# Twelve tiny loads of x among the last large loads of a decode step

## The chip, the cores and the metric

The kernel runs on one core of a Trainium2 chip. The core has a matrix engine (TensorE, PE in the profile), three engines for element-wise work (VectorE, DVE; ScalarE, ACT; GpSimd, POOL), a sync engine (SyncE, SP) that here does nothing but issue loads, and 16 DMA engines that move bytes from the chip's memory into the on-chip buffer. The metric is the device time of one execution in microseconds (us), as a median over runs.

## What is computed

One token `x` of 576 numbers is normalised and sent through two branches, whose results are added to it.

```python
xn = _layernorm(x)
return x + _A_ref(xn, k_cache, v_cache, wq, wo) + _B_ref(xn, w_in, w_sp, b_sp, w_out)
```

Branch A is attention for one query: `q = xn @ wq` gives 32 heads of 128; there are 16 key/value heads, so two query heads share one; only the last 4,096 positions of the cache of 65,536 are looked at; the softmax of the scores weighs the values, and the result (4,096 numbers) is multiplied by `wo`. Branch B is a gated MLP: `z = gelu(xn @ w_in)` gives 4,608 numbers, the second half is normalised, scaled and shifted by two scalars, multiplied with the first half, and multiplied by `w_out`. All inputs are bf16.

Every weight and every key and value is used once. The kernel must read 16 MiB of keys, 16 MiB of values and some 17 MB of weights, 50.96 MB by the profile.

## The kernel before

**The loads.** All large loads are issued by SP, in the order in which the code lists them, and land in a ring of seven buffers (`ring`, 20,736 bytes in each of 128 partitions): `wq` in three pieces, the keys of two pairs of heads, `w_in` in three pieces, then keys and values in turn (`K[m]`, `V[m]`, 2 MiB each, for m of 0 to 7), then `w_out` in one load (`wout`, L95), then `wo` in five loads of 14, 9, 6, 2 and 1 of its 32 slices (L95 again). Every one of these loads fills 128 partitions with one contiguous piece each. A load into a ring buffer is issued when the load seven places before it has been consumed, so SP waits for PE or DVE before most of them. SP works strictly in order: what stands behind a waiting load waits too.

**Small loads.** ACT issues three small loads at the start (`xrow`, x as one row of 1,152 bytes; two scalars of 2 bytes into `spb`, side by side in one tile) and the store of the result at the end.

**Completion signals.** Each load tells of its landing through a semaphore. The semaphores named in the trace's records show eight of them, used in turn by all loads of SP and ACT in their order in the program. Before a load takes a semaphore that the eighth load before it used, its issuer waits until that earlier load has landed.

**The work between.** Keys are transposed on DVE (`kT`, L268), scores are made on PE (`S`, L277), the maximum, exponential and sum run on DVE and ACT (L298 to L321), and the weighted sum of the values on PE (`ops`, L344). This is done in four groups of four key/value heads. `zps` (L380) is branch B's first product. The tail is `out_mms` (L467): two accumulators `acc`, each over half of the 576 output columns, take 18 slices of `w_out` and then the 32 slices of `wo`, two multiplications a slice. Then `res` is copied out of the accumulators (L492, L493), and ACT stores it (L494).

The order of all instructions is that of the code (`manual_schedule`); nothing is moved by a planner. What sets the order around the change is SP's queue alone:

```python
wout_sb = load_n(B_w_out, NF, 0, NF, "wout")
wo_sb = []
for n in (14, 9, 6, 2, 1):
    wo_sb += load_n(A_wo, 32, len(wo_sb), n, "wo")
```

In the following, "wo14", "wo9", "wo6", "wo2" and "wo1" are these five loads, and V4 to V7 and K5 to K7 the last values and keys.

Of the kernel before, what the change touches and what calls it, by code (L numbers as in the profile page):

```python
# [9 lines left out]
BF16 = mybir.dt.bfloat16  # L10
# [29 lines left out]
def kernel(  # L40
# [14 lines left out]
    nc = tc.nc  # L55
# [5 lines left out]
    const = ctx.enter_context(tc.tile_pool(name="const", bufs=1))  # L61
# [10 lines left out]
    x_flat = A_x.flatten_outer_dims()  # L72


    def ring_tile(name, rows, width):
        t = ring.tile([P, SLOT], BF16, name=name, tag="ring")
        return t[:, 0:rows * width].rearrange("p (s c) -> p s c", c=width)
# [8 lines left out]
    def load_kv(src, m, name):  # L86

        t = ring.tile([P, SLOT], BF16, name=f"{name}{m}", tag="ring")
        v = t[:, 0:TP * DH]
        nc.sync.dma_start(v, src[0, 2 * m:2 * m + 2, SK - W:SK, :].rearrange("h (r t) d -> r h (t d)", t=TP))  # L90
        return v.rearrange("p (t d) -> p t d", d=DH)

    def load_n(src, per, lo, n, name):
        v = ring_tile(f"{name}{lo}", n, D)
        nc.sync.dma_start(v, src.rearrange("(p t) n -> p t n", t=per)[:, lo:lo + n, :])  # L95
        return [(lo + t, v[:, t, :]) for t in range(n)]
# [8 lines left out]
        V[m - 2] = load_kv(A_v_cache, m - 2, "v")  # L105
    for m in range(NP - 2, NP):
        V[m] = load_kv(A_v_cache, m, "v")
    wout_sb = load_n(B_w_out, NF, 0, NF, "wout")
    wo_sb = []
    for n in (14, 9, 6, 2, 1):  # L110
        wo_sb += load_n(A_wo, 32, len(wo_sb), n, "wo")


# [315 lines left out]
    for j in range(2 * NP):  # L429
        g, o = divmod(j, GK)  # L430
# [94 lines left out]
```

## Time and profile before

| what | value |
|---|---|
| median of 3 runs | 127.33 us (127.26 to 127.34) |
| span of the profiled execution, first to last instruction | 125.4 us |
| time of that execution outside its span | not recorded; the median is 1.9 us over the span |
| read from memory | 50.96 MB, 406 GB/s over the span |
| PE, DVE, ACT, POOL busy | 68.4, 78.5, 33.6, 7.9 us |
| loads issued by SP | 24, in 128 rows each, of 0.14 to 2.6 MB |
| DMA packets on SP's queue | 4,032 |

The profile shows one execution: the busy time of every engine, the span in 40 slices, the DMA queues, and the chain of work that ended last. Its DMA line gives the mean busy share of the 16 DMA engines, so a value a little under full can mean that all are nearly full or that some are done and others are not. Behind the views lie records of single DMA packets (start, duration, size, queue) and of every semaphore update; they do not name the DMA engine.

### The profile page before, as it was taken

The page shows a single profiled execution, that of the slowest core. Times are in us where ns is not written, and L with a number is a line of the kernel's source. Part 1 is how long each engine was busy: PE and PEld are TensorE (multiplying, and loading weights), DVE is VectorE, ACT ScalarE, POOL GpSimd, SP SyncE. Part 2 cuts the span into 40 slices and gives each one's busy share as a digit, 9 for nine tenths or more (in the row PEclk, how much of TensorE's full clock was granted, in tenths as well). Part 3 has the DMA queues.
Part 4 walks back from the last instruction along what each step waited for, and adds up shares of the span by engine and source line. Part 5 has one row for each costly group of instructions (what it writes and reads, how often), then busy time and mean ns, then how long its engine had stood idle before and what let it go on. Part 6 is the DMA issues. An engine that isn't in the chain of part 4 may idle for free.

```text
span 125.4 us, 1630 instructions
## 1 busy us (share of the span) xinstructions
PE 68.4 (55%) x626; PEld 31.4 (25%) x626; DVE 78.5 (63%) x150; ACT 33.6 (27%) x85; POOL 7.9 (6%) x27
## 2 busy tenths in 40 slices
PE   0034810398999668069257049639029811178862
PEld 0021110112699612014011012411003511024640
DVE  6853049997517595794798298899098967005001
ACT  4000030000072950000441940260860092920001
POOL 2991000000000000100000000000000000000000
PEclk9999995558975555959958977986955996557998
DMA  4999999999999999999999999999999999999960
GB/s 115 455 423 422 425 434 439 422 428 435 428 438 418 434 434 428 423 444 423 428 439 434 413 439 434 428 428 434 428 436 434 428 426 439 434 409 427 416 261 0
DMA packets 4047, 51.06 MB, mean 407 GB/s; under 512 B 454, under 2 KB 584, under 8 KB 840
## 3 DMA queue, kind: packets, MB, share of 16 engines
q1 hardware_dynamic: 4032, 50.96, 95.6%
q8 instruction: 5, 0.08, 0.2%
q14 instruction: 2, 0.02, 0.0%
q10 hardware_dynamic: 8, 0.00, 0.0%
HBM read 50.96 MB, written 0.00 MB: 406 GB/s over the span
## 4 chain that ended last, share of the span: by engine, by line
DMA 71%; PE 11%; DVE 11%; issue 2%; SPq 1%; ACT 1%
DMA k<-in_A_k_cache_dram 44%; DMA wo<-in_A_wo_dram 17%; DMA wq<-in_A_wq_dram 10%; DVE kT L268 6%; PE S L277 5%; PE ops L344 3%; DVE Qb L255 2%; PE qps L227 1%; PE acc L467 1%; DVE q_rep L238 1%; ACT q_rep L236 1%; DVE on L358 1%; PE lps L327 1%; SPq L83 1%; DVE om L354 1%
## 5 line engine op out<-in xcount | busy, mean ns | idle before, releaser
L277 PE MATMUL S<-kT,Qb 128*8 128x512 bf16 x128 | 32.3, 636 | 30.3 <-DVE kT L268 30.3
L268 DVE STREAM_TRANSPOSE kT<-k 128x1024 f32<-128x1024 f32 x32 | 36.9, 1212 | 8.3 <-DMA k<-in_A_k_cache_dram 8.3
L305 ACT ACTIVATE pz<-S,nm 64x1024 bf16<-64x1024 f32 x8 | 11.2, 1406 | 45.0 <-DVE nm L301 30.3
L321 ACT COPY PT<-pt 32x64 f32<-32x64 f32 x64 | 18.9, 295 | 14.6 <-DVE pt L315 13.8
L277 PEld LDWEIGHTS <-Qb 128*8 128x8 bf16 x128 | 6.4, 96 | 49.7 <-issue 46.7
L344 PE MATMUL ops<-v,PT 128*16 128x512 bf16 x128 | 11.7, 441 | 3.5 <-ACT PT L321 3.5
L315 DVE STREAM_TRANSPOSE pt<-pz 128x1024 bf16<-128x1024 bf16 x8 | 9.4, 1212 | 4.1 <-ACT pz L305 4.1
L380 PEld LDWEIGHTS <-win 128*128 128x128 bf16 x162 | 10.1, 165 | 0.9 <-issue 0.9
L380 PE MATMUL zps<-XT,win 128*128 128x2 bf16 x162 | 10.2, 201 | 0.0
L354 DVE SCALAR_TENSOR_TENSOR om<-ops,rs,dmask 128x512 f32<-128x512 f32 x4 | 3.0, 742 | 7.4 <-PE ops L344 7.3
L298 DVE TENSOR_REDUCE mx<-S 128x1 f32<-128x1024 f32 x4 | 4.9, 1220 | 3.7 <-PE S L277 3.7
L344 PEld LDWEIGHTS <-PT 128*16 128x16 bf16 x128 | 5.0, 97 | 7.3 <-ACT PT L321 4.1
L227 PE MATMUL qps<-wq,XT 128*2 128x512 bf16 x36 | 4.2, 621 | 2.3 <-DVE XT L218 1.9
L467 PE MATMUL acc<-wo,Y 128*1 128x288 bf16 x64 | 4.6, 285 | 1.3 <-DMA wo<-in_A_wo_dram 1.3
L236 ACT CAST q_rep<-qps 128x512 bf16<-128x512 f32 x2 | 1.2, 585 | 14.0 <-DVE q_rep L238 14.0
L238 DVE CAST q_rep<-qps 128x512 bf16<-128x512 f32 x2 | 1.4, 692 | 5.1 <-PE qps L227 4.5
L193 PE MATMUL ps_x<-ones_b,xtw 1*128 1x1 bf16 x9 | 0.4, 162 | 7.2 <-DVE xtw L191 7.2
L492 DVE CAST res<-acc 1x288 bf16<-1x288 f32 x1 | 0.4, 446 | 6.1 <-PE acc L467 6.1
L358 DVE TENSOR_REDUCE on<-om 128x128 f32<-128x512 f32 x4 | 4.1, 1034 | 0.1
L327 PE MATMUL lps<-lx,lsum 128*128 128x1 f32 x8 | 2.1, 333 | 3.2 <-DVE Y L372 3.2
L493 ACT CAST res<-acc 1x288 bf16<-1x288 f32 x1 | 0.4, 389 | 12.4 <-PE acc L467 12.4
L467 PEld LDWEIGHTS <-Y 128*1 128x1 bf16 x64 | 2.9, 83 | 3.0 <-issue 1.9
(90 smaller groups left out, 46.8 us busy)
## 6 DMA issues: line engine op xcount, KB each, us to landing
k<-in_A_k_cache_dram SPq DMA_DIRECT2D x8, 2048.0 KB, 27.2
v<-in_A_v_cache_dram SPq DMA_DIRECT2D x8, 2048.0 KB, 27.8
win<-in_B_w_in_dram SPq DMA_DIRECT2D x3, 1728.0 KB, 27.1
wout<-in_B_w_out_dram SPq DMA_DIRECT2D x1, 2592.0 KB, 30.2
wq<-in_A_wq_dram SPq DMA_DIRECT2D x1, 2048.0 KB, 9.3
wo<-in_A_wo_dram SPq DMA_DIRECT2D x1, 2016.0 KB
wq<-in_A_wq_dram SPq DMA_DIRECT2D x1, 1536.0 KB, 12.5
wo<-in_A_wo_dram SPq DMA_DIRECT2D x1, 1296.0 KB
```

Of the source, the lines that this page charges most:

```text
L227: nc.tensor.matmul(qps[32 * g:32 * g + 2, :], lhsT=XT[:, s, :], rhs=wv[:, 512 * g:512 * (g + 1)], start=(s == 0), stop=(s == NS - 1), tile ...
L268: nc.vector.transpose(dst[:, 1024 * n:1024 * (n + 1)], src[:, 1024 * n:1024 * (n + 1)])
L277: nc.tensor.matmul(S[g % 2][32 * i:32 * i + 8, hf, :], lhsT=Qb[:, 2 * m + hd, be].rearrange("p a h -> p (a h)"), rhs=kv[:, be // 2, be % 2 ...
L298: nc.vector.tensor_reduce(out=mx[:, 0:1], in_=s[:], op=ALU.max, axis=mybir.AxisListType.XY)
L305: nc.scalar.activation(p[lo:hi, :, :, hd], s[lo:hi].rearrange("p a (t r) -> p (a t) r", r=16), ACT.Exp, bias=nm[lo:hi, 0:1], scale=SCALE, ...
L315: nc.vector.transpose(dst[:, 1024 * n:1024 * (n + 1)], src[:, 1024 * n:1024 * (n + 1)])
L321: nc.scalar.copy(PT4[32 * a:32 * a + 32, i % 2, i // 2, :], pt4[32 * i:32 * i + 32, :, a])
L344: nc.tensor.matmul(ops[32 * q:32 * q + 16, :], lhsT=d["PT"][:, pr, t0:t0 + 4].rearrange("p t x h -> p (t x h)"), rhs=V[2 * g + pr][:, t0:t ...
L354: nc.vector.scalar_tensor_tensor(out=om[:].rearrange("p c d -> p (c d)"), in0=ops[:], scalar=d["rs"][:, 0:1], in1=dmask[:].rearrange("p c ...
L358: nc.vector.reduce_sum(on[:], om[:].rearrange("p c d -> p d c"), axis=AXX)
L380: nc.tensor.matmul(zps[:, :, t], lhsT=wt[:, t, :], rhs=XT[:, s, :], start=(s == 0 and t == 0), stop=(s == NS - 1 and t == NF - 1), skip_gr ...
L467: nc.tensor.matmul(acc[n], lhsT=lhs[:, col:col + 1], rhs=wv[:, CW * n:CW * (n + 1)], start=False, stop=last, tile_position=(0, 32 * n))
```

## The change

A tile `mk` of 16 partitions is added, and twelve loads that fill parts of it from `x`. A load "of k rows" cuts the first k(23 + k) numbers of x into k rows of 23 + k numbers, and writes them into k partitions, at a column of their own. They are issued on SP's queue: those of 15, 14 and 13 rows ahead of `wout`; those of 12, 11, 10 and 9 between `wout` and wo14; those of 8, 7, 6, 4 and 2 between wo14 and wo9. Nothing reads `mk`. They hold 111 rows and 7,516 bytes together, and a row has 50 to 76 bytes.

```diff
     for m in range(NP - 2, NP):
         V[m] = load_kv(A_v_cache, m, "v")
+    mk = const.tile([16, 16 * 40], BF16, name="mk")
+
+    def rows_of_x(ks):
+        for k in ks:
+            n = 23 + k
+            nc.sync.dma_start(mk[0:k, 40 * k:40 * k + n], x_flat[:, 0:k * n].rearrange("o (k n) -> (o k) n", n=n))
+
+    rows_of_x((15, 14, 13))
     wout_sb = load_n(B_w_out, NF, 0, NF, "wout")
-    wo_sb = []
-    for n in (14, 9, 6, 2, 1):
+    rows_of_x((12, 11, 10, 9))
+    wo_sb = load_n(A_wo, 32, 0, 14, "wo")
+    rows_of_x((8, 7, 6, 4, 2))
+    for n in (9, 6, 2, 1):
         wo_sb += load_n(A_wo, 32, len(wo_sb), n, "wo")
```

## The prediction

> **What bounds the kernel now.** I read the page's slices and queues first, then the chain that ended last.
>
> ```profile
> DMA  4999999999999999999999999999999999999960
> q1 hardware_dynamic: 4032, 50.96, 95.6%
> q8 instruction: 5, 0.08, 0.2%
> q10 hardware_dynamic: 8, 0.00, 0.0%
> DMA 71%; PE 11%; DVE 11%; issue 2%; SPq 1%; ACT 1%
> ```
>
> The DMA engines are full from the second slice to the last but two; SP's queue (q1) alone takes 95.6% of them. No compute engine is near that, so the time is bytes over rate, plus a head and a tail. The tail is the place of the change, so I cut it finely (columns: stretch, length, busy time of PE, PEld, DVE, ACT, POOL, clock, DMA share, GB/s).
>
> ```profile
> 100.00:110.00 10.00, 1.77 (x16) 0.92 (x12) 5.00 (x10) 7.00 (x18) 0.00 (x0) 0.71 1.01 432
> ...
> 120.50:121.00 0.50, 0.23 (x4) 0.03 (x1) 0.00 (x0) 0.00 (x0) 0.00 (x0) 1.00 0.88 321
> 121.00:121.20 0.20, 0.00 (x0) 0.00 (x0) 0.00 (x0) 0.00 (x0) 0.00 (x0) 1.00 0.30 110
> 121.20:121.60 0.40, 0.07 (x2) 0.07 (x3) 0.00 (x0) 0.00 (x0) 0.00 (x0) 1.00 0.33 127
> 121.60:122.00 0.40, 0.40 (x8) 0.28 (x9) 0.00 (x0) 0.00 (x0) 0.00 (x0) 1.00 0.25 92
> 122.00:122.30 0.30, 0.30 (x10) 0.18 (x6) 0.00 (x0) 0.00 (x0) 0.00 (x0) 1.00 0.18 61
> ```
>
> From 121.0 on, about a quarter to a third of the DMA engines still work: eleven are done and five are late. The records of single packets say who. The 16 completions of the last load, wo1, arrive at 120.88 to 121.52 for eleven engines, at 121.92 for one and at 122.45, 122.53, 122.55 and 122.62 for four. Followed back, each late engine lost its time in one step, when an instruction fetch ran on it: the 16 KB fetches at 32.4, 42.9, 70.2 and 102.3 cost their engines some 0.95 us each, and smaller ones some 0.3. PE starts its last pair of multiplications at 122.66, 0.04 us behind the last completion. So **four late DMA engines set the end, and eleven have about 1.1 us to spare**.
>
> ```profile
> 100.24 21.25 DMA wo<-in_A_wo_dram
> 121.49 0.04 issue
> 121.53 1.46 PE acc L467 x18
> 122.99 0.43 DVE res L492
> ```
>
> This chain leaves the DMA with wo6's landing, at 121.49, but inside its PE piece PE waits for wo2 and wo1 too.
>
> **The change part by part.** Nothing is removed. Added are 12 loads (111 rows, 7,516 bytes), and `wout` and the five `wo` loads move behind them on SP's queue. ACT's and POOL's queues are not touched, though ACT's last store takes its semaphore in a later turn.
>
> *Time on the DMA engines.* The nearest rows are ACT's scalars of 2 bytes, which ran between the packets of a full engine. There, 16,384-byte packets follow each other every 607 ns, and every 613 where one small packet came between, data or completion alike: 6 ns a packet. A row of 68 bytes adds 68 / 27.0 GB/s (16,384 bytes in 607 ns) = 2.5 ns. So a row and a completion cost 6 + 2.5 + 6 = 14.5 ns on its engine. How a load of 15 rows is divided over engines no row shows. If all ran on one late engine, 123 packets x 6 ns + 7,516 bytes / 27.0 = 0.74 + 0.28 = 1.0 us at the end; if all ran on early engines, nothing, under their 1.1 us. I take the even division, because every large load puts 9 packets on each of 16 engines: 111 / 16 = 7 rows x 14.5 ns = **0.10 us**, on the late engines too, and so at the end. A dearer packet is possible: ACT's row of 1,152 bytes took 47 ns up to its completion; with that price, 47 + 6 = 53 ns x 12 loads = 0.64 us on an engine that takes part in all.
>
> The Trainium skill, "DMA: Bandwidth & Descriptors", section "Why a DMA increments its semaphore by 16 and not by 1", says that a load of k rows (k up to 16) runs on the lowest-numbered k engines. By it engines 0 and 1 would take 12 rows each, 0.17 us, and engine 15 none; the end would move by 0 to 0.17, by the numbers of the late engines, which no record here gives. Engine 0 by that rule is the one with ACT's single-row packets, and in this trace it is the second earliest at wo1, 1.27 us ahead of the last: the rule makes the forecast's cost smaller if anything.
>
> *Issue on SP.* Small loads on ACT cost 0.21 and 0.27 us of issue, the first one 0.51.
>
> ```profile
> 0.74 0.51 ACTq L115 DMA_DIRECT2D xrow<-in_A_x_dram  x1
> 1.28 0.21 ACTq L117 DMA_DIRECT2D spb<-in_B_w_sp_dram  x1
> 1.52 0.27 ACTq L118 DMA_DIRECT2D spb<-in_B_b_sp_dram  x1
> ```
>
> With 0.3 each, waits' overhead included, 12 cost 3.6 us of SP, which has nothing else to do; the cover is the backlog of the queue, from issue to landing 20 us and more. If it were gone, the 3.6 us would lie on the path.
>
> *New waits.* Eight semaphores go round over the loads. `win`'s second load shows the price: its ring buffer was free, and yet SP waited 1.4 us, for `wq`'s first load, eight loads before.
>
> ```profile
> SPq L83 <- DMA wq<-in_A_wq_dram: 1.4, 1, 1.4
> SPq L95 <- DMA k<-in_A_k_cache_dram: 4.7, 1, 4.7
> ```
>
> Twelve more loads in the round put each large load eight places behind a much younger one. I count on: the 15, 14 and 13 rows wait for K5, V3 and K6, landed by 81.13, so they go at 81.4; `wout` waits for V4 (85.97, before: issued at 81.39); 12, 11, 10 and 9 rows wait for K7, V5, V6 and V7 (90.8, 95.7, 100.5, 105.39); wo14 goes at 105.8 (before 85.80); 6 rows wait for `wout` itself (111.58); after them and the 4 and 2 rows, three issues of 0.3, wo9 goes at 112.5 (before 95.52) and wo6 at 112.9; wo2 waits for wo14 (116.35), and wo1 follows at 116.8 (before 113.88). An issue reaches the engines 0.9 to 1.0 us after it begins (`xrow` 0.74 to 1.64, `wq` 0.73 to 1.73). Needed, on the earliest engine, are: wo14 at 109.5, wo9 at 114.3, wo6 at 117.4, wo2 at 119.5, wo1 at 120.4. The closest is wo9: 113.4 against 114.3, **0.9 us to spare**; wo14 has 2.8, wo2 2.1 and wo1 2.6. Nobody but the loads waits for SP, so these waits cost 0.
>
> Other parts: the 1.3 KB of `mk` in the buffer and the ACT store's turn cost 0; the store's semaphore was last used by the 7 rows, landed 6 us before it.
>
> The sum is 0.10 us. The profiled span is 125.43, the median 1.90 above it; what lies around the span doesn't change, so 125.53 in the profile and **127.43** in the median.
>
> **The rivals.**
>
> *Dearer packets.* Up to 53 ns a load on engines that do nothing between: +0.3 to +0.64, 127.6 to 128.0. For it: no trace has 15 engines reading the same 1,152 bytes at once, and three completions in a row on one ring. Against: 2-byte packets cost 6 ns beside a full stream. The even load's whole gain is lost from 0.25 us on, that is 36 ns a load on a late engine with seven.
>
> *SP too late.* If a small load costs SP far more than on ACT, wo9 comes late. A late engine needs wo9 at 116.0; an early one that starts it at 116.2 ends with them (it needs 6.1 us to the end). So it decides from 116.2, an issue at 115.3, 3.7 us after `wout`'s landing: 1.2 us for each small load. At 1.5 us each the end moves by 0.9: 128.2.
>
> *One after the other.* If each small load has to land before the next is issued (one tile `mk`), twelve latencies come into the queue; the store's 1.1 us (123.50 to 124.60) x 12 gives up to 13 us, 140. Against it: the two loads into `spb` were issued 0.24 us apart, the first landing at 5.25. The same page, in its section "Rules for kernel authors", calls transfers under 64 KB mostly overhead, and gives some 2 us of fixed cost to each; by it 12 in turn would be 24 us. The trace shows such latencies to overlap.
>
> *Faster.* If the 16 engines share a limit, the early ones' time on small packets is the late ones' gain: their lag of 1.1 us would shrink. It decides from 0.25 us over the last 37 us, 0.7% in pace, 607 to 603 ns a packet. At a third of the lag: 126.95. Against it: a late engine's 2,304-byte packets follow at 89 ns both with 16 engines at work and with five.
>
> **How the numbers follow.** Forecast 0.48, dearer packets 0.22, SP late 0.12, one after the other 0.06, faster 0.12. 0.2% (0.25 us) is about what a measurement of this kernel can tell from no change. The forecast lies within it, and a fifth of the dearer packets: same 0.52; slower 0.18 + 0.12 + 0.06 = 0.36; faster 0.12. The range leaves out the serial case and most of the faster one, and ends above SP late at 1.5 us a load: 127.15 to 128.3. The forecast's own is 127.33 to 127.55.
>
> **What would show it.** After: 12 more issues on SP, `wout` issued near 86, wo14 near 105.8, wo9 near 112.5, wo1 near 116.8; DMA share still 1.01 until 120; 111 packets under 100 bytes of some 9 ns; the eleven-and-five picture 0.1 us later. A DMA share under 0.98 between 105 and 119 would be SP late; a late group that moves by over 0.25 us with full engines is dearer packets. The prediction is wrong if a wait I did not count holds SP, or if instruction fetches fall on other engines.

## The result, and the profile after

The changed kernel takes 127.99 us (127.79 to 128.14, 4 runs) against 127.30 (127.24 to 127.34, 4 runs) of the kernel before: a ratio of 1.0055, 95% interval 1.0039 to 1.0071. It is slower by 0.69 us, inside the stated range, but beyond the forecast of 127.43, which was "no change that can be measured". In the experiments below, one run of e6 (129.56 us), over 1.5% above the fastest of its kernel, counts as slow and is left out of its ratio.

The page of the changed kernel, its slices and queues and the shares of the chain that ended last:

```profile
span 125.9 us, 1642 instructions
DMA  3999999999999999999999999999999999999960
q1 hardware_dynamic: 4254, 50.96, 95.5%
DMA 78%; DVE 8%; PE 8%; SPq 2%; issue 2%; ACT 1%
```

The DMA engines are as full as before. SP issues 28 loads before (the table above says 24; 28 x 144 packets make its 4,032) and 40 after. SP's queue has 222 packets more, twice 111: each row came with a completion of its own. The end of the transfers, cut as before:

```profile
120.50:121.00 0.50, 0.47 (x8) 0.19 (x5) 0.00 (x0) 0.00 (x0) 0.00 (x0) 1.00 1.00 389
121.00:121.20 0.20, 0.00 (x0) 0.00 (x0) 0.00 (x0) 0.00 (x0) 0.00 (x0) 1.00 0.94 357
121.20:121.60 0.40, 0.00 (x0) 0.00 (x0) 0.00 (x0) 0.00 (x0) 0.00 (x0) 1.00 0.58 202
121.60:122.00 0.40, 0.23 (x4) 0.17 (x5) 0.00 (x0) 0.00 (x0) 0.00 (x0) 1.00 0.26 104
122.00:122.30 0.30, 0.30 (x10) 0.21 (x6) 0.00 (x0) 0.00 (x0) 0.00 (x0) 1.00 0.28 100
```

The early eleven engines, done at 121.0 before, now work on to 121.4, but from 121.6 on the picture is that of before: a quarter of the engines is late. wo1's last completion came at 122.78, 0.16 later than the 122.62 of before. The span grew by 0.43 (125.43 to 125.86), and the median by 0.69. So 0.27 of the loss lies between the last load and the last instruction, and 0.26 outside the span altogether; the other 0.16 is wo1's lateness, which is taken up again below.

The 0.27 is seen in SP's checks at the end of the program, the same kind of row in both kernels (times are those of the first and last start). First before, then after:

```profile
L520 SPq EVENT_SEMAPHORE  x7: 17/28/825, 119.4 to 125.4; - x7
```

```profile
L530 SPq EVENT_SEMAPHORE  x7: 17/28/28, 124.8 to 125.8; - x7
```

By the semaphore records, SP checks the eight load semaphores and two others at its end, in five instructions, two in each, in the same order in both kernels. Each that follows another costs 0.065 us. Before, the store of the result used the semaphore that is checked last: four checks were done from 119.4 on, while the last loads landed, and only the store's own was left. With twelve more loads in the round, the store takes the semaphore that is checked first. SP stands there until 124.78 and does the four other checks behind it. From the store's landing to the end of the span it took 0.83 us before (124.60 to 125.43) and 1.10 after (124.76 to 125.86).

### The profile page after: what moved, and what is told of

It reads as the page before. It is cut to its first block, busy times and chain, and to the rows that moved or that the text cites. A ratio compares the mean times of both kernels' runs of the same rounds, so it can differ in the third digit from the quotient of the medians.

```text
span 125.9 us, 1642 instructions
## 1 busy us (share of the span) xinstructions
PE 68.3 (54%) x626; PEld 31.5 (25%) x626; DVE 78.5 (62%) x150; ACT 33.6 (27%) x85; POOL 7.9 (6%) x27
## 4 chain that ended last, share of the span: by engine, by line
DMA 78%; DVE 8%; PE 8%; SPq 2%; issue 2%; ACT 1%
DMA k<-in_A_k_cache_dram 21%; DMA wout<-in_B_w_out_dram 20%; DMA v<-in_A_v_cache_dram 20%; DMA wq<-in_A_wq_dram 10%; DMA wo<-in_A_wo_dram 7%; DVE kT L278 5%; PE S L287 3%; DVE Qb L265 2%; PE ops L354 2%; PE qps L237 1%; DVE q_rep L248 1%; PE acc L477 1%; ACT q_rep L246 1%; SPq L113 1%; SPq L83 1%
## 5 line engine op out<-in xcount | busy, mean ns | idle before, releaser
L331 ACT COPY PT<-pt 32x64 f32<-32x64 f32 x64 | 18.9, 295 | 14.5 <-DVE pt L325 13.7
```

The lines of the kernel that those rows point to most:

```text
L331: nc.scalar.copy(PT4[32 * a:32 * a + 32, i % 2, i // 2, :], pt4[32 * i:32 * i + 32, :, a])
```

## The experiments

All put loads of the same pieces of x into `mk` (one of them takes rows of `w_out`). "Behind the store" is the number of checks that follow the one of the store; "end" is from the store's landing to the end of the span in the profiled run; "outside" is time less span, the mean over the runs.

| kernel | small loads on SP | behind the store | end | outside | median | ratio (95%) |
|---|---|---|---|---|---|---|
| before, again (e1) | 0 | 0 | 0.84 | 1.81 | 127.32 | 0.9996 (0.9987 to 1.0005) |
| the change | 12 | 4 | 1.10 | 2.08 | 127.99 | 1.0055 (1.0039 to 1.0071) |
| e2, one row each | 12 | 4 | 1.09 | 2.08 | 127.87 | 1.0060 (1.0035 to 1.0085) |
| e3, one row each | 8 | 0 | 0.83 | 1.82 | 127.44 | 1.0004 (0.9996 to 1.0013) |
| e4, 15 to 8 rows | 8 | 0 | 0.83 | 1.83 | 127.35 | 1.0003 (0.9994 to 1.0011) |
| e5, one row each | 4 | 4 | 1.09 | 1.83 | 127.60 | 1.0022 (1.0013 to 1.0031) |
| e6, the change and 4 early | 16 | 0 | 0.83 | 1.85 | 127.60 | 1.0028 (1.0012 to 1.0045) |
| e7, 128 rows each | 8 | 0 | 0.83 | 1.82 | 128.01 | 1.0057 (1.0044 to 1.0069) |
| e8, the change, 4 moved early | 12 | 4 | 1.10 | 2.09 | 127.90 | 1.0047 (1.0033 to 1.0060) |
| e9, one row each | 14 | 2 | 0.95 | 2.11 | 127.79 | 1.0033 (1.0021 to 1.0046) |
| e10, nine ahead of wo9 | 16 | 0 | 0.83 | 1.84 | 131.41 | 1.0317 (1.0296 to 1.0339) |
| e11, four more on ACT | 8 | 4 | 1.09 | 1.80 | 128.76 | 1.0120 (1.0097 to 1.0142) |
| e12, one row each | 10 | 3 | 1.00 | 1.84 | 127.47 | 1.0011 (1.0002 to 1.0020) |

### Packets, checks or a late queue?

The kernel before once more (no edit), for its spans:

> The kernel before once more, beside itself, for the span of each run. If the time outside the span is the same in both kernels (2.05 to 2.1 us in the runs of the changed kernel, 127.95 - 125.9 among them), the spans here are 125.2 to 125.3; if the changed kernel also pays outside its span, they are 125.4 and 1.9 lies outside. Ratio 1.000.

All twelve loads in their places, but of one row, and the same with eight of them; then the change with eight:

```diff
-            nc.sync.dma_start(mk[0:k, 40 * k:40 * k + n], x_flat[:, 0:k * n].rearrange("o (k n) -> (o k) n", n=n))
+            nc.sync.dma_start(mk[0:1, 40 * k:40 * k + n], x_flat[:, 0:n])     # e2, e3
...
-    rows_of_x((8, 7, 6, 4, 2))
+    rows_of_x((8,))     # e3, e4
```

> The twelve loads at the same places, but each of one row, so all their packets run on one engine, which is an early one. Theory A (the row packets on late engines cost 0.1 us, and the store's semaphore, now checked first of five at the end, costs 0.27): the last large load lands as before, the end still takes 1.10 us from the store's landing, so +0.27 in the span, 127.6. Theory B (all of the loss is the packets on the late engines): 127.3. Theory C (SP's late issue of wo9 costs the loss): as the changed kernel, 128.0.

> As the run before with the last four loads left out, so that the store's semaphore is again the last that is checked, and wo9 goes on SP right behind wo14. Theory A: 0.83 us from the store's landing to the end, 127.3 to 127.35. Theory B: 127.3. Theory C: 127.3. A cost per added load, wherever it lies: two thirds of what twelve cost.

> The changed kernel with the loads of 7, 6, 4 and 2 rows left out: the store's semaphore is the last one checked, wo9 is early, and the late engines have 1 to 8 small loads each. Theory A: +0.08 for packets, nothing at the end, 127.4. Theory B: nearly all of the loss stays, since nearly all packets stay (92 of 111 rows): 127.85. Theory C: 127.3.

e2 keeps nearly all of the loss (127.87) with 12 row packets instead of 111; e4 loses nothing that can be measured with 92 rows. So the rows are not the loss: theory B falls. Theory A's 1.10 and 0.83 us came as expected, but e2 stands 0.27 above its 127.6. That is the time outside the span: 2.08 us in e2 and in the change, 1.81 in the kernel before. I had taken it for fixed.

### The store's turn alone, and the time outside the span

e5 is e2 with only the 15, 14, 13 and 12 (as one row each); e6 is the change and four one-row loads behind the keys' fourth to seventh load:

```diff
         K[m] = load_kv(A_k_cache, m, "k")
+        if m in (3, 4, 5, 6):
+            k = (5, 3, 1, 0)[m - 3]
+            nc.sync.dma_start(mk[0:1, 40 * k:40 * k + 23 + k], x_flat[:, 0:23 + k])
```

> Only four one-row loads (ahead of wout three, behind it one). Nothing of them runs on a late engine, wo9 goes on SP behind wo14 at once, but the store takes the semaphore that is checked first of five at the end, as with twelve. Theory A1 (the store's turn is the whole loss): 1.10 us from the store's landing to the end of the span, and 2.05 outside it, so 127.8 as with twelve. Theory A2 (the turn costs 0.27 in the span, and the 0.2 outside it goes with the number of loads or of SP's instructions): 127.55. Theory D (the loss goes with the number of loads alone, none up to eight): 127.3.

> The whole change (twelve loads, 111 rows, wo9 as late on SP) and four one-row loads more, one each behind the keys' fourth to seventh load, so that the store again takes the semaphore that is checked last. Theory A1: all but the packets' 0.1 us comes back, 127.4. Theory A2: 127.6. Theory C (SP's late issue of wo9) or D (number of loads): 128.0 or more.

Both agree with A2 in the store's turn. Four one-row loads at a harmless place cost 0.29 us (127.60 against 127.31), and nearly all of it is the checks. Sixteen loads (e6), the whole change among them, bring the store back to the last check, and the end with it; the time outside came back too. That e6's median is still the 127.6 of A2 is chance: A2 put 0.2 us of it outside the span, and in e6 it lies inside. Without its three runs above 128 the median is 127.49. The checks of e5, e6 and e4, one row of each profile:

```profile
L529 SPq EVENT_SEMAPHORE  x7: 17/28/28, 124.7 to 125.7; - x7
```

```profile
L532 SPq EVENT_SEMAPHORE  x7: 17/28/825, 119.6 to 125.5; - x7
```

```profile
L530 SPq EVENT_SEMAPHORE  x7: 17/28/825, 119.6 to 125.5; - x7
```

Where the first check starts at 124.7, the store holds it and four stand behind; where it starts at 119.6, they were done while loads landed.

The outside time did not follow A2's "number of loads": 1.85 with sixteen, 2.08 with twelve. Four runs went after it. e8 moves four of the twelve loads (7, 6, 4 and 2 rows) behind the keys' fourth to seventh load; e9 and e12 have e3's eight and six or two one-row loads among the keys; e11 has e3's eight and four on ACT's queue:

```diff
     nc.scalar.dma_start(spb[:, 1:2], B_b_sp.flatten_outer_dims()[0:1, 0:1])
+    for k in (7, 6, 4, 2):
+        nc.scalar.dma_start(mk[0:1, 40 * k:40 * k + 23 + k], x_flat[:, 0:23 + k])
```

> All twelve loads of the change, but the 7, 6, 4 and 2 rows one each behind the keys' fourth to seventh load, so that wo9 goes on SP behind wo14 at once. The store's semaphore is checked first of five, as in the change. Theory A3 (in the span: 0.27 for the store's turn, 0.1 for packets; outside the span 0.25 that belongs to twelve loads): 127.9, with 2.07 outside, and no run far above the others. Theory E (the 0.25 outside comes from where the loads stand, or from SP's late issue): 127.65, with 1.82 outside. Theory C2 (SP's late issue of wo9 is what gives runs of 128.5 to 129.7): none here.

> Fourteen one-row loads, eight at places of the change and six one each behind the keys' third to eighth load. The store takes the third of the five checks, so two stand behind it: 0.83 + 2 x 0.065 = 0.96 us from its landing to the end, 127.45 if 1.82 lies outside the span. If the time outside grows from twelve loads on, 2.07 outside and 127.7; if it belongs to twelve alone, 1.82 to 1.85.

> Twelve one-row loads, eight on SP's queue at places of the change and four on ACT's queue at the start. The store's semaphore is checked first of five: 1.10 us from its landing to the end of the span. Theory G (the 0.25 outside the span goes with the length of SP's program): 1.82 outside, 127.6. Theory H (it goes with the number of loads, whoever issues them): 2.08 outside, 127.85.

> Ten one-row loads on SP's queue, two of them behind the keys' fifth and sixth load. The store takes the second of the five checks, three stand behind it: 0.83 + 3 x 0.065 = 1.03 us from its landing to the end. Outside the span 1.82 if the step comes between ten and twelve loads (127.5), 2.08 if between eight and ten (127.75).

The time outside is 1.80 to 1.85 with 0, 4, 8, 10 and 16 added loads on SP, and 2.08 to 2.11 with 12 and 14, wherever they stand (e8) and whatever their rows (e2). With eight on SP and four on ACT it is 1.80 (e11): so it goes with the loads that SP itself issues, not with the number of all loads. The records of e6, e9 and e10 (16, 14 and 16) hold one 8 KB instruction fetch more, 1.6 to 1.9 us behind the end of the span; those with fewer loads hold none there.

The semaphore records narrow the place. In the 0.37 us ahead of the span they are alike in all kernels, and the last one stands 1.90 to 1.91 us behind the span's end in the kernel before, e1, the change, e2 and e8. So the 0.26 lies behind that last one, or more than 0.37 ahead of the span. One group of them, the updates of semaphores 207 to 255, starts 0.65 to 0.66 us behind the end with 0 to 10 added loads on SP, 0.68 to 0.69 with 12 and 14, and 1.19 to 1.21 with 16, where the last updates come no later for it. So one step behind the span does move with the number of loads on SP. A wait of SP for the next block of its program would fit, but no row shows it, and no run made SP's program longer without adding loads: it stays an argument. The Trainium skill, "Runtime: NRT & Kernel Launch", section "Instruction fetch mechanics", says that programs are fetched in blocks while the current one runs, and that crossing a boundary is mostly hidden. Whether the 0.26 us is such a crossing no run here shows; the instruction fetches in the records are of 8 KB on one queue and of 16 KB on another.

The ends of e9 and e12, 0.95 and 1.00 us with two and three checks behind the store, lie near 0.83 + 0.065 each (0.96 and 1.03). Four places of the store (0, 2, 3 and 4 checks behind it) thus show the price of a check.

e11 held a surprise: it lost 1.1 us more than the checks cost. The four loads on ACT shift the round, so that `wq`'s third load comes eight places behind its first. SP's waits in the first 10 us of e11:

```profile
SPq L83 <- DMA wq<-in_A_wq_dram: 3.0, 1, 3.0
SPq L83 <- DMA xrow<-in_A_x_dram: 1.0, 1, 1.0
```

That load was issued at 5.50 instead of 1.62 and landed at 15.26 instead of 14.07, and the queue ran at 370 GB/s between 5 and 10 us, where it ran at 418 before.

### What does a packet cost, and a late load?

e7 has eight loads of 128 rows of 76 bytes at e4's places, so that all 16 engines carry 8 rows and a completion of each:

```diff
-            nc.sync.dma_start(mk[0:k, 40 * k:40 * k + n], x_flat[:, 0:k * n].rearrange("o (k n) -> (o k) n", n=n))
+            nc.sync.dma_start(mk[:, 40 * k:40 * k + 38], B_w_out[0:128, 0:38])
```

> Eight loads at the places of eight of the twelve, each of 128 rows of 76 bytes (from w_out), so that each of the 16 engines, the late ones too, has 8 rows and a completion of each load. The store's semaphore is the last one checked. By the prices of the trace, (8 x (6 + 2.8) + 6) ns = 76 ns a load, 0.6 us for eight, all at the end: 127.9. If a packet of this kind costs more than its time in the stream, over that; if the late engines do not set the end, 127.3.

It took 128.01, +0.70, 88 ns a load where 76 were worked out. From V7's landing to wo1's, the mean of the four latest completions grew from 17.19 to 17.21 us (the runs with no or one-row loads) to 17.80: 0.60, or 75 ns a load. Packets on the late engines do come out at the end, at about the price of the stream.

e10 puts nine one-row loads between wo14 and wo9:

```diff
-    rows_of_x((8, 7, 6, 4, 2))
+    rows_of_x((8, 7, 6, 5, 4, 3, 2, 1, 0))     # one row each, as in e2
```

> Nine one-row loads between wo14 and wo9, so wo9 stands eight places behind wo14 itself or nearly so, and one small load before it has to wait for wo14's landing (116.4): wo9 is issued at about 116.8. The store's semaphore is the last one checked. Theory C2 (a load needs about 2.1 us from issue to the end of its first packet on an emptied queue, 112.78 to 115.2 in the changed kernel): the queue is empty from 114.4, the first packets of wo9 end near 119, and 6.1 us of work stand behind that: +2.4 in the span, 129.7. If an issue reaches the engines in 0.9 us, as the prediction had it: +1.3, 128.6.

It took 131.41, +4.1 (its profiled run 130.94, with a span 3.7 longer than before). wo9 was issued at 117.21, and the queue ran empty (window rows of e10):

```profile
114.00:116.00 2.00, 2.00 (x26) 1.10 (x19) 1.79 (x2) 0.00 (x0) 0.00 (x0) 0.57 0.35 145
116.00:118.00 2.00, 2.00 (x44) 1.51 (x42) 0.20 (x1) 0.00 (x0) 0.00 (x0) 1.00 0.00 0
118.00:120.00 2.00, 0.70 (x12) 0.36 (x9) 0.00 (x0) 0.00 (x0) 0.00 (x0) 1.00 0.91 270
122.00:126.00 4.00, 3.28 (x28) 1.86 (x29) 0.00 (x0) 0.00 (x0) 0.00 (x0) 0.57 0.81 326
```

Nothing but the last two small rows moved for two microseconds. The first packets of wo9 started at 118.18, 0.97 us after the issue, as the prediction had it, but took 0.52 to 1.38 us instead of 0.39, so the first data was in 1.5 to 2.3 us after the issue. Theory C2 is right in kind and short in size: wo1 landed 3.2 us late (125.80), where +2.4 was expected. PE added half a microsecond: the store was issued 1.42 us behind that landing instead of 0.89, at a granted clock of 0.57 between 122 and 126.

The changed kernel has a small piece of this. In the window rows of before and after (the same two stretches) the engines idle a little just where wo9 begins:

```profile
114.30:114.90 0.60, 0.60 (x14) 0.41 (x10) 0.60 (x1) 0.00 (x0) 0.00 (x0) 0.89 0.99 421
114.90:115.50 0.60, 0.60 (x14) 0.33 (x8) 0.57 (x2) 0.00 (x0) 0.00 (x0) 1.00 0.98 419
```

```profile
114.30:114.90 0.60, 0.60 (x8) 0.38 (x6) 0.60 (x1) 0.00 (x0) 0.00 (x0) 0.50 0.91 309
114.90:115.50 0.60, 0.60 (x14) 0.39 (x12) 0.57 (x2) 0.00 (x0) 0.00 (x0) 0.99 0.91 350
```

wo9 was issued at 112.78, and its first packets on the early engines took up to 0.8 us instead of 0.39. Only engines with 1.1 us to spare pay it; e8, which issues wo9 six microseconds earlier and is the change otherwise, takes 127.90 against 127.99, and 127.87 in e2. So the late issue costs nothing that can be told in most runs. But among the kernels that issue wo9 so late, e2 and e6 had 4 of 23 runs (that of 129.56 not counted), of 128.17 to 129.67, that stand above their median by 0.5 us or more (the change itself none of 4); e1, e3 to e5, e7 to e9 and e12 had none of 70. What delays those runs was not recorded, so it is not shown that the late issue does it.

## Why the prediction was right in range and wrong in its likeliest case

**What bounds the kernel: right.** The late engines set the end before and after, and what was put on all engines in e7 came out at the end.

**Time on the DMA engines: right in size.** 0.10 us was taken. In the medians it can't be told from zero. The profiled run has wo1 0.16 later, but its late engines were on average 0.11 late at the landing of V7 already, ahead of the first small packet; in the medians, e4 with 92 of the rows is 0.05 above its kernel before, e3 with eight rows is 0.14 above. The records tell more than the medians. From V7's landing to wo1's, the mean of the four latest completions took 17.19 to 17.21 us in eight runs with no or one-row loads (before, e1, e2, e3, e5, e9, e11, e12), and 17.24 to 17.29 in the four with full rows (the change, e4, e6, e8): 0.03 to 0.10 us. In a train, that is the small loads that follow each other between two large ones, row and completion mostly take 13 to 14 ns, against 14.5. The Trainium skill's rule on k rows and k engines ("DMA: Bandwidth & Descriptors", section "Why a DMA increments its semaphore by 16 and not by 1") agrees with the records, as far as records without engine numbers can show it: 111 rows brought 111 completions, and in each train an engine with a row of a small load has one of every larger load too. (The second earliest completion of wo1 before is at 120.90, which is 1.72 us ahead of the last and not 1.27.)

**Issue on SP and new waits: right.** `wout` was issued at 86.13 (86.0 predicted), wo14 at 105.98 (105.8), wo9 at 112.78 (112.5), wo1 at 117.05 (116.8). This is the whole of SP's list from 105 to 118 us (start, length, count; a length runs from the first to the last of a merged group):

```profile
105.61 0.27 SPq L113 DMA_DIRECT2D mk<-in_A_x_dram  x1
105.98 0.35 SPq L95 DMA_DIRECT2D wo<-in_A_wo_dram  x1
106.38 6.30 SPq L113 DMA_DIRECT2D mk<-in_A_x_dram  x5
112.78 4.67 SPq L95 DMA_DIRECT2D wo<-in_A_wo_dram  x4
```

The **0.9 us to spare** for wo9 were wrong. The step counted to the start of the first packet and not to its end, which an emptied queue delays by up to 1 us more. The rival "SP too late" was therefore nearer than it was priced, and stayed covered by the early engines' slack alone. Its sign, a DMA share under 0.98 between 105 and 119, did appear (0.97 from 115 to 119), but the kernel before stands at 0.98 there itself, and the end did not follow; the sign could not tell the two apart.

**"The ACT store's turn cost 0": wrong.** This is the step that failed. I looked at what the store has to wait for, and not at who waits for the store's semaphore: SP's checks at the end, whose order is fixed. It measured 0.27 us.

**"What lies around the span doesn't change": wrong.** It grew by 0.26 us. That needed a comparison of time and span in runs with other numbers of loads on SP, which the profile of before does not have. Where the step is was narrowed above; its cause stays open.

So 0.27 + 0.26 + up to 0.1 for packets make the 0.69 within its interval of 0.5 to 0.9. That the range held it was luck: its upper part was there for dearer packets and for SP too late, and the loss came from two terms put at 0. None of the rivals was the cause: packets were not dearer, SP was not too late in most runs, and the loads into `mk` did not wait for each other (three issued within 1.1 us, from 81.35 to 82.42).

## What to carry to other kernels

When loads are added or removed, count on to the end of the program which semaphore the last transfer gets and how many checks follow it: here every check behind it cost 0.065 us, and a number of added loads that is a multiple of eight left it where it was. Compare time minus span between kernels too, since part of a loss may lie where no row of the trace is. And for a load that is to follow without a gap, count to the end of its first packet and not to its start: on the empty queue of e10 that end came 1.5 to 2.3 us after the issue.

## What the runs showed of the hardware that was not expected

- A load's place in the round of eight semaphores can cost far more than its bytes: four one-row loads at the start (e11) delayed the issue of another load by 3.9 us, its landing by 1.2 and the end by about 1.1.
- With 12 and 14 loads added on SP, some 0.26 us are added outside the span; with 10 and fewer, and again with 16, they are not.
- A small load in a full stream costs its engines about 14 ns for row and completion, though alone it takes far longer to land: in e10 a one-row load issued on the empty queue at 116.59 landed at 117.75.
